# Start-up of a fused attention and MoE kernel: two heads normed first, four weight units loaded first, and an uneven share of W3O

## The chip, the cores and the metric

The kernel runs on one core of a Trainium2 chip. The metric is device time in microseconds (us) of one execution. A core has a matrix engine (TensorE, PE in the profile, with its weight loads as PEld), three elementwise engines (VectorE or DVE, ScalarE or ACT, GpSimd or POOL), and SyncE (SP), whose queue issues nearly all DMA transfers here. Each engine works through its own instructions in a fixed order.

## The reference

```python
q_n, k_n = rmsnorm(q, g_q), rmsnorm(k, g_k)      # q, k, v: (4, 12, 448, 64)
attn = softmax(q_n @ k_n.T / 8)
x = (attn @ v) -> (1792, 768)                    # heads side by side
g = relu(x @ w_in) ** 2                          # w_in 768 x 2048
x = g @ w_out                                    # w_out 2048 x 768
h = ((x @ w1) * (x @ w2)) @ w3                   # w1, w2 768 x 1024, w3 1024 x 1024
out = h @ w_out2                                 # 1024 x 768
```

## The kernel before

The kernel walks over 48 heads (4 batches of 12). `NH`, `H` and `GH` are 48, 12 and 4. For each head it prepares K and Q (`head_prep`, `stage_k`), makes scores in two halves of two 112-row blocks (`stage_qk`), takes the exponential (`stage_exp`), transposes the result (`stage_t`, `stage_lo`) and multiplies by V (`stage_v`). The norms of four heads are made together as a group (`load_group`, `group_prep`); only the first group is cut up. PE would be idle in much of a head, so the loop calls `fill(n)` six times a head, and each call runs matrix products of another job until `n` matmuls are paid for.

During heads 0 to 12 that other job is W3O, the product of w3 and the last weight matrix (`gen_w3o`). It is 8 x 2 x 8 = 128 groups of three matmuls (`mm3`, lines 262 to 264; a high and a low part of each operand make three). From head 13 on it is the MoE chain of the batch whose attention is done, with three such matmuls a group too.

The weights arrive as 64-bit values in units of 128 x 384 or 128 x 512. A unit is loaded by SP (`load_next`, L180) into one of four buffers `raw64`, worked on by ACT (L194) and by POOL or ACT (L200, L198), joined into 32 bits by DVE (L207), which frees the `raw64` buffer, and split into a high part by ACT (L106) and a low part by POOL or, one in five, by DVE (L114). The tiles of a split unit are called `hl`, `x` or `act` in the profile, by the pool that they borrow. The first 16 groups of W3O (`ic` = 0) need 16 units of the last weight matrix (`wo`) and two of w3, a new unit for nearly every group; each 16 groups after them need two units of w3. `advance` keeps loading up to five units ahead of the one in use, as far as the `raw64` buffers allow.

SP's queue is one queue in a fixed order: a load that waits for its buffer holds up all behind it. `qt`, the transposed Q of a head, has two buffers, and a buffer comes free when DVE has made `ql` (L497) of the head that used it.

The scheduler of the framework puts the instructions of each engine into their order when the kernel is built, by the order in the program and by what it expects to be ready, so an instruction can stand earlier or later than its place in the program.

Of the kernel before, what the change touches and what calls it, by code (L numbers as in the profile page):

```python
# [29 lines left out]
def attention_moe_kernel(  # L30
# [15 lines left out]
    nc = tc.nc  # L46
    B, P, H, C, D = q_nat.shape
    S = P * C
    NH = B * H
    GH = 4  # L50
# [5 lines left out]
    NIC = w3t.shape[0] // 2  # L56
# [114 lines left out]
    def is64(i):  # L171
        return units[i][0].dtype != F32
# [14 lines left out]
    def load_to(i):  # L187
        while pos["load"] <= min(i, NU - 1) and is64(pos["load"]):
            load_next()
# [200 lines left out]
    def load_group(g):  # L390
        if not (0 <= g < NH // GH):
            return
        b, h0 = divmod(g * GH, H)
        qn = t1.tile([P, GH, C, D], F32, name="qn", tag="qn")
        kn = t2.tile([P, GH, C, D], F32, name="kn", tag="kn")
        if g == 0:
            nc.sync.dma_start(out=kn[:, 0:1], in_=k_nat[0, :, 0:1])
            load_head(0)
            nc.sync.dma_start(out=qn[:, 0:1], in_=q_nat[0, :, 0:1])
            load_to(0)  # L400
            nc.sync.dma_start(out=kn[:, 1:], in_=k_nat[0, :, 1:GH])
            nc.sync.dma_start(out=qn[:, 1:], in_=q_nat[0, :, 1:GH])
            load_to(1)
        else:
            nc.sync.dma_start(out=kn, in_=k_nat[b, :, h0:h0 + GH])
            nc.sync.dma_start(out=qn, in_=q_nat[b, :, h0:h0 + GH])
        grp[g] = [qn, kn, None, None]

    def load_head(h):
        if not (0 <= h < NH):  # L410
            return
        b, hh = divmod(h, H)
        t = t2.tile([128, S], F32, name="qt", tag="qt")
        nc.sync.dma_start(out=t, in_=q_t[b, hh])
        qts[h] = t
# [22 lines left out]
    def group_prep(g):  # L438
        if not (0 <= g < NH // GH):
            return  # L440
        qn, kn = grp[g][:2]
        n = GH * C
        if g == 0:
            sq = hlp.tile([128, 1024], F32, name="sq", tag="hl")[:P].rearrange("p (h c d) -> p h c d", h=GH, c=C)
        else:
            sq = qn
        ss = small.tile([P, 2, n], F32, name="ss", tag="ss")
        rr = grp[g][2] = t2.tile([P, 2, n], F32, name="rr", tag="rr")

        def sums(i, x, sq, a, b):  # L450
            nc.scalar.activation(out=sq[:, a:b], in_=x[:, a:b], func=AF.Square)
            t = sq[:, a:b].rearrange("p h c d -> p (h c) d")
            nc.vector.tensor_reduce(out=ss[:, i, a * C:b * C], in_=t, axis=AX.X, op=ALU.add)

        def norm(i, j, a, b):
            s = ss[:, i:j, a * C:b * C]
            nc.vector.tensor_scalar(out=s, in0=s, scalar1=1.0 / D, scalar2=1e-6, op0=ALU.mult, op1=ALU.add)
            return rsqrt(rr[:, i:j, a * C:b * C], s)

        if g == 0:  # L460
            sums(1, kn, sq, 0, 1)
            first.enter_context(tc.issue_after(norm(1, 2, 0, 1)))
            head_prep(0)
            stage_k(0)
            sums(0, qn, qn, 0, 1)
            norm(0, 1, 0, 1)
            sums(1, kn, sq, 1, GH)
            sums(0, qn, qn, 1, GH)
            norm(0, 2, 1, GH)
        else:  # L470
            sums(0, qn, qn, 0, GH)
            sums(1, kn, sq, 0, GH)
            norm(0, 2, 0, GH)

    def head_prep(h):
        if not (0 <= h < NH):
            return
        g, i = divmod(h, GH)
        _, kn, rr, _ = grp[g]
        kx = t1.tile([P, C, D], F32, name="kx", tag="kx")  # L480
        nc.gpsimd.tensor_tensor(
            out=kx, in0=kn[:, i], in1=rr[:, 1, i * C:(i + 1) * C].unsqueeze(2).to_broadcast([P, C, D]), op=ALU.mult
        )
        khl = t2.tile([P, C, 2 * D], F32R, name="khl", tag="khl")
        copy_on(KHI_ENG[h // H], khl[:, :, :D], kx)
        sub_on(KLO_ENG[h // H], khl[:, :, D:], kx, khl[:, :, :D].bitcast(F32))
        qt = qts.pop(h)
        qh = t2.tile([128, S], F32R, name="qh", tag="qh")
        ql = t2.tile([128, S], F32R, name="ql", tag="ql")
        qe = QHI_ENG[h // H]  # L490
        if qe == "a":
            nc.scalar.activation(out=qh, in_=qt, func=AF.Copy, scale=gg[:, 0:1])
        else:
            ENGS[qe].tensor_scalar(
                out=qh, in0=qt, scalar1=gg[:, 0:1], scalar2=1.0, op0=ALU.mult, op1=ALU.mult
            )
        nc.vector.scalar_tensor_tensor(  # L497
            out=ql, in0=qt, scalar=gg[:, 0:1], in1=qh.bitcast(F32), op0=ALU.mult, op1=ALU.subtract
        )
        heads[h] = dict(khl=khl, qh=qh, ql=ql, rq=rr[:, 0, i * C:(i + 1) * C], p=[None] * C, pt={}, lo=[])  # L500
# [145 lines left out]
    def start_fill(gen, total):  # L646
        state.update(gen=gen, credit=0.0, left=total)

    def fill(n):
        state["credit"] += n  # L650
        while state["gen"] is not None and state["credit"] > 0:
            try:
                k = next(state["gen"])
                state["credit"] -= k
                state["left"] -= k
            except StopIteration:
                state["gen"] = None

    MOE = 3 * (NFC * KX + 2 * NE * KF + 2 * NJ * KX + NE * NIC)
    W3O = 3 * 2 * NIC * NIC  # L660

    nc.scalar.preload_act_table_set("natural_log_exp_and_others")
    nc.sync.dma_start(out=g_sb, in_=g_in)
    load_group(0)
    load_head(1)
    make_identity(nc, ident)
    nc.vector.tensor_copy(out=ident_r, in_=ident)
    nc.vector.scalar_tensor_tensor(
        out=gg, in0=g_sb[:, 0:1], scalar=float(D) ** -0.5, in1=g_sb[:, 1:2], op0=ALU.mult, op1=ALU.mult
    )  # L670
    first = ExitStack()
    group_prep(0)
    load_head(2)
    head_prep(1)
    load_v(0)
    start_fill(gen_w3o(), W3O)
    first.close()
    for h in range(NH + 1):
        n = W3O / ((H + 1) * 6) if h <= H else MOE / (H * 6)
        load_head(h + 3)  # L680
        load_v(h + 1)
        if h % GH == 0:
            load_group(h // GH + 1)
        stage_qk(h, 0)
        fill(n)
        stage_exp(h, 0)
        if h % H != 1:
            stage_x(h - 2)
        stage_t(h - 1, 0)
        stage_t(h - 1, 1)  # L690
        fill(n)
        stage_lo(h - 1)
        if h < NH:
            v_prep(h)
        fill(n)
        stage_k(h + 1)
        stage_t(h - 1, 2)
        stage_t(h - 1, 3)
        fill(n)
        stage_lo(h - 1)  # L700
        stage_qk(h, 1)
        fill(n)
        stage_exp(h, 1)
        fill(n)
        stage_v(h - 1)
        if h % GH == 1:
            group_prep(h // GH + 1)
        head_prep(h + 2)
        if h and h % H == 0:
            fill(1e9)  # L710
            stage_x(h - 1)
            start_fill(gen_moe(h // H - 1), MOE)
    fill(1e9)
# [56 lines left out]
```

## Time and profile before

| | us |
|---|---|
| median of 3 runs (1233.05 to 1234.97) | 1234.19 |
| the profiled execution | 1230.67 |
| its span (first to last instruction) | 1228.6 |
| PE busy | 1162.9 (95%) |
| POOL busy | 781.5 (64%) |
| ACT busy | 732.0 (60%) |
| DVE busy | 689.0 (56%) |

The profiled execution is one run of its own; 2.07 us of its time lie outside the span. A busy share is an average over stages, and the stages differ: in the first 58.91 us PE is busy for 33.39 us.

### The profile page before, as it was taken

Reading aid. Unit: us, or ns where it says so; the run is one execution under the profiler, and the core shown is the slowest. Engines: PE = TensorE matmul, PEld = TensorE weight load, DVE = VectorE, ACT = ScalarE, POOL = GpSimd, SP = SyncE. Lnnn points to the kernel's source line nnn. Section 1 sums busy time; section 2 is a strip of 40 time slices with the busy share of each in tenths; the row PEclk is TensorE's granted clock in tenths of the full one; section 3 lists DMA queues with packets and bytes.
Section 4 is the critical chain, followed back from the end, with each engine's and each line's share of the span. In section 5 each row is a group of like instructions: output and inputs, shape, how many; then the busy total and the mean of one; then the engine's idle time right before and its main releaser. Section 6 shows DMA issues by size and latency. Waiting matters only on the chain.

```text
span 1228.6 us, 18882 instructions
## 1 busy us (share of the span) xinstructions
PE 1162.9 (95%) x6192; PEld 1050.8 (86%) x6192; DVE 689.0 (56%) x1230; ACT 732.0 (60%) x1581; POOL 781.5 (64%) x772
## 2 busy tenths in 40 slices
PE   4798999997988899999999999999999999999998
PEld 3587888886877799998998999999999999999998
DVE  5798888759978773556566554645655421012100
ACT  6898877767657565656646556656555544443442
POOL 5884425665676664756776664846766556678673
PEclk9799999999999999999999999999999999999999
DMA  7785457888788865545545455444543443333342
GB/s 224 246 256 158 146 148 237 271 290 251 256 254 261 245 192 172 146 131 150 159 114 167 134 168 164 140 133 136 153 123 114 138 138 114 110 113 103 104 125 75
DMA packets 111346, 207.63 MB, mean 169 GB/s; under 512 B 12208, under 2 KB 66704, under 8 KB 111248
## 3 DMA queue, kind: packets, MB, share of 16 engines
q1 hardware_dynamic: 107792, 200.92, 54.2%
q10 hardware_dynamic: 3456, 5.51, 1.2%
q8 instruction: 49, 0.80, 0.3%
q14 instruction: 49, 0.40, 0.1%
HBM read 149.95 MB, written 27.53 MB: 144 GB/s over the span
## 4 chain that ended last, share of the span: by engine, by line
PE 69%; DMA 10%; DVE 8%; ACT 5%; POOL 4%; issue 3%; SPq 1%; DVEq 0%; POOLq 0%; ACTq 0%
PE mm L262 19%; PE mm L263 19%; PE mm L264 19%; PE pt L571 4%; PE kv L623 3%; DMA raw<-w_out 2%; PE sc L525 2%; DMA raw<-w 2%; DMA pw<-p 2%; PE sc L526 2%; ACT p L544 2%; DMA raw<-w_in 2%; DVE nb L527 1%; POOL hl L114 1%; DVE raw L207 1%
## 5 line engine op out<-in xcount | busy, mean ns | idle before, releaser
L114 POOL TENSOR_TENSOR hl<-raw,hl 128x384 fp32r<-128x384 f32 (+1 forms) x383 | 446.3, 1169 | 261.3 <-ACT hl L106 250.8
L106 ACT ACTIVATE hl<-raw 128x384 fp32r<-128x384 f32 (+1 forms) x416 | 233.6, 564 | 148.8 <-PE mm L264 86.4
L262 PE MATMUL mm<-x,hl 128*128 128x448 f32 (+1 forms) x832 | 309.6, 372 | 1.4 <-DVE gf L334 1.4
L263 PE MATMUL mm<-x,hl 128*128 128x448 f32 (+1 forms) x832 | 305.9, 368 | 4.5 <-POOL x L114 4.4
L264 PE MATMUL mm<-x,hl 128*128 128x448 f32 (+1 forms) x832 | 304.9, 366 | 3.4 <-DVE hl L114 1.9
L263 PE MATMUL mm<-act,hl 128*128 128x448 f32 (+1 forms) x640 | 235.8, 368 | 3.2 <-POOL act L114 2.3
L262 PE MATMUL mm<-act,hl 128*128 128x448 f32 (+1 forms) x640 | 238.1, 372 | 0.0
L264 PE MATMUL mm<-act,hl 128*128 128x448 f32 (+1 forms) x640 | 234.5, 367 | 0.7 <-DVE hl L114 0.7
L544 ACT ACTIVATE p<-sc,nb,rr 112x448 f32<-112x448 f32 x192 | 137.5, 720 | 76.6 <-DVE nb L528 74.4
L263 PEld LDWEIGHTS mm<-x,hl 128*128 128x128 f32 x832 | 157.6, 189 | 19.2 <-POOL x L114 7.1
L264 PEld LDWEIGHTS mm<-x,hl 128*128 128x128 f32 x832 | 157.7, 189 | 17.2 <-DVE hl L114 2.3
L262 PEld LDWEIGHTS mm<-x,hl 128*128 128x128 f32 x832 | 157.8, 190 | 15.1 <-DVE gf L334 1.8
L527 DVE TENSOR_REDUCE nb<-sc 112x1 f32<-112x448 f32 x192 | 113.4, 615 | 40.3 <-PE sc L526 38.6
L263 PEld LDWEIGHTS mm<-act,hl 128*128 128x128 f32 x640 | 121.7, 190 | 14.6 <-POOL act L114 4.0
L264 PEld LDWEIGHTS mm<-act,hl 128*128 128x128 f32 x640 | 121.7, 190 | 10.7 <-DVE hl L114 1.1
L262 PEld LDWEIGHTS mm<-act,hl 128*128 128x128 f32 x640 | 121.7, 190 | 9.7
L114 DVE TENSOR_TENSOR ptr<-pt,ptr 128x448 fp32r<-128x448 f32 x144 | 86.8, 619 | 72.8 <-ACT ptr L106 72.0
L200 POOL TENSOR_SCALAR raw<-raw 128x384 uint32<-128x384 uint16 (+1 forms) x110 | 81.2, 739 | 64.5 <-DMA raw<-w_in 23.8
L207 DVE SCALAR_TENSOR_TENSOR raw<-raw 128x384 uint32<-128x384 uint32 (+1 forms) x120 | 82.7, 694 | 42.8 <-POOL hl L114 28.5
L114 POOL TENSOR_TENSOR act<-gf,act 128x448 fp32r<-128x448 f32 x80 | 97.1, 1214 | 7.6 <-ACT act L106 3.4
L194 ACT ACTIVATE raw<-raw 128x384 f32<-128x384 f32 (+1 forms) x120 | 70.6, 599 | 50.8 <-DMA raw<-w 17.6
L334 DVE TENSOR_TENSOR gf<-mm,r 128x448 f32<-128x448 f32 x64 | 39.8, 621 | 96.0 <-ACT r L330 95.4
(84 smaller groups left out, 1578.6 us busy)
## 6 DMA issues: line engine op xcount, KB each, us to landing
pw<-p SPq DMA_DIRECT2D x72, 392.0 KB, 4.3
raw<-f_in SPq DMA_DIRECT2D x96, 192.0 KB, 2.4
raw<-f_out SPq DMA_DIRECT2D x72, 256.0 KB, 2.7
raw<-f SPq DMA_DIRECT2D x96, 192.0 KB, 2.4
raw<-w_in SPq DMA_DIRECT2D x32, 384.0 KB, 4.5
raw<-w_out SPq DMA_DIRECT2D x24, 512.0 KB, 5.9
raw<-w SPq DMA_DIRECT2D x32, 384.0 KB, 5.0
raw<-w3o SPq DMA_DIRECT2D x48, 256.0 KB, 2.8
```

The costliest lines, as they stand in the source:

```text
L106: nc.scalar.activation(out=out, in_=in_, func=AF.Copy)
L114: e.tensor_tensor(out=out, in0=in0, in1=in1, op=ALU.subtract)
L194: nc.scalar.activation(out=hi, in_=hi, func=AF.Prelu, scale=2.0**-112, alpha=-(2.0**32))
L200: nc.gpsimd.tensor_scalar(out=t[:, :n, 0], in0=low, scalar1=2.0**-13, scalar2=2.0**-14 - 0.5, op0=ALU.mult, op1=ALU.add)
L207: nc.vector.scalar_tensor_tensor(out=f[:, :n].bitcast(U32), in0=t[:, :n, 1], scalar=3, in1=t[:, :n, 0], op0=ALU.logical_shift_left, op1=AL ...
L262: nc.tensor.matmul(ps, w[:, 0, wk, :], x[0], start=(i == 0), stop=False)
L263: nc.tensor.matmul(ps, w[:, 0, wk, :], x[1], start=False, stop=False)
L264: nc.tensor.matmul(ps, w[:, 1, wk, :], x[0], start=False, stop=(i == last))
L334: nc.vector.tensor_tensor(out=gf, in0=ps, in1=r, op=ALU.mult)
L527: nc.vector.tensor_reduce(out=nb[:, j:j + 1], in_=o[j], axis=AX.X, op=ALU.max, negate=True)
L544: nc.scalar.activation(out=p, in_=o[j], func=AF.Exp, scale=d["rq"][:, c:c + 1], bias=nb[:, j:j + 1], accum_out=sm[:, i, c:c + 1],)
L571: nc.tensor.transpose(to[:kn, c * P:(c + 1) * P], d["p"][c][:, k0:k0 + kn], one)
```

## The change

In the first group, K and Q of heads 0 and 1 are loaded as one piece and normed together (before: head 0 alone, then heads 1 to 3). The `qt` load of head 1 and the first `wo` unit go ahead of K and Q of heads 2 and 3, and two more `wo` units are loaded right behind those. `head_prep(1)` moves ahead of the norm of the later heads. Head 0 gets no W3O in its first four `fill` calls and four groups in its last two; head 1 gets 8 groups, head 2 gets 9, and heads 3 to 12 get 10.7 each. Before, each of the 13 heads got 9.85.

```diff
         if g == 0:
-            nc.sync.dma_start(out=kn[:, 0:1], in_=k_nat[0, :, 0:1])
+            nc.sync.dma_start(out=kn[:, 0:2], in_=k_nat[0, :, 0:2])
             load_head(0)
-            nc.sync.dma_start(out=qn[:, 0:1], in_=q_nat[0, :, 0:1])
+            nc.sync.dma_start(out=qn[:, 0:2], in_=q_nat[0, :, 0:2])
             load_to(0)
-            nc.sync.dma_start(out=kn[:, 1:], in_=k_nat[0, :, 1:GH])
-            nc.sync.dma_start(out=qn[:, 1:], in_=q_nat[0, :, 1:GH])
+            load_head(1)
             load_to(1)
+            nc.sync.dma_start(out=kn[:, 2:], in_=k_nat[0, :, 2:GH])
+            nc.sync.dma_start(out=qn[:, 2:], in_=q_nat[0, :, 2:GH])
+            load_to(3)
...
         if g == 0:
-            sums(1, kn, sq, 0, 1)
-            first.enter_context(tc.issue_after(norm(1, 2, 0, 1)))
+            sums(1, kn, sq, 0, 2)
+            first.enter_context(tc.issue_after(norm(1, 2, 0, 2)))
             head_prep(0)
             stage_k(0)
-            sums(0, qn, qn, 0, 1)
-            norm(0, 1, 0, 1)
-            sums(1, kn, sq, 1, GH)
-            sums(0, qn, qn, 1, GH)
-            norm(0, 2, 1, GH)
+            sums(0, qn, qn, 0, 2)
+            norm(0, 1, 0, 2)
+            head_prep(1)
+            sums(1, kn, sq, 2, GH)
+            sums(0, qn, qn, 2, GH)
+            norm(0, 2, 2, GH)
...
+    GROUPS = [4, 8, 9] + [(2 * NIC * NIC - 21) / (H - 2)] * (H - 2)
...
     load_group(0)
-    load_head(1)
...
     load_head(2)
-    head_prep(1)
     load_v(0)
...
-        n = W3O / ((H + 1) * 6) if h <= H else MOE / (H * 6)
+        n = 3 * GROUPS[h] / (6 if h else 2) if h <= H else MOE / (H * 6)
...
         stage_qk(h, 0)
-        fill(n)
+        if h:
+            fill(n)
         stage_exp(h, 0)
...
         stage_t(h - 1, 1)
-        fill(n)
+        if h:
+            fill(n)
...
             v_prep(h)
-        fill(n)
+        if h:
+            fill(n)
...
         stage_t(h - 1, 3)
-        fill(n)
+        if h:
+            fill(n)
         stage_lo(h - 1)
         stage_qk(h, 1)
         fill(n)
```

## Rows read from the trace of the kernel before

**Rows 1.** Page, part 2: PE busy tenths in 40 slices of 30.7 us

```profile
PE   4798999997988899999999999999999999999998
```

**Rows 2.** Windows by stage: length, then busy us per engine, clock, DMA share, GB/s

```profile
0.00:12.00 12.00, 0.71 (x4) 0.56 (x4) 6.41 (x18) 6.66 (x14) 3.95 (x11) 1.00 0.80 227
12.00:31.00 19.00, 12.56 (x38) 8.67 (x38) 11.12 (x24) 12.70 (x30) 14.09 (x19) 1.00 0.68 223
31.00:58.91 27.91, 20.12 (x73) 15.62 (x73) 21.40 (x34) 22.79 (x48) 24.01 (x22) 0.76 0.80 256
58.91:72.85 13.94, 13.94 (x85) 12.71 (x85) 13.06 (x23) 12.85 (x30) 12.03 (x14) 1.00 0.84 236
72.85:176.00 103.15, 95.31 (x586) 84.98 (x585) 86.64 (x170) 84.47 (x190) 51.77 (x67) 1.00 0.55 167
```

**Rows 3.** Waits of POOL from 7 to 59 us: total, times, longest

```profile
POOL raw L200 <- DMA raw<-wo: 4.1, 3, 1.7
POOL hl L114 <- ACT hl L106: 3.0, 2, 1.5
```

**Rows 4.** Timeline of SP's queue from 4 to 32 us: start, duration, what

```profile
4.00 0.43 SPq L180 DMA_DIRECT2D raw<-wo  x1
...
8.26 0.43 SPq L405 DMA_DIRECT2D kn<-k_nat  x1
13.48 0.34 SPq L414 DMA_DIRECT2D qt<-q_t  x1
...
14.34 1.38 SPq L180 DMA_DIRECT2D raw<-wo  x3
15.81 0.38 SPq L180 DMA_DIRECT2D raw<-w3t  x1
25.19 2.70 SPq L180 DMA_DIRECT2D raw<-wo  x3
```

**Rows 5.** Timeline of DVE from 4 to 17 us

```profile
4.20 0.42 DVE L453 TENSOR_REDUCE ss<-sq 112x4 f32<-112x256 f32 x1 [1.53 <-ACT sq L451]
...
9.68 0.95 DVE L453 TENSOR_REDUCE ss<-sq 112x12 f32<-112x768 f32 x1
...
12.78 0.68 DVE L497 SCALAR_TENSOR_TENSOR ql<-qt,gg,qh 128x448 fp32r<-128x448 f32 x1
13.37 1.25 DVE L431 TENSOR_TENSOR nt<-rr 112x24 f32<-112x24 f32 x1
...
16.12 0.18 DVE L435 TENSOR_TENSOR rr<-nt,rr 112x24 f32<-112x24 f32 x1
```

**Rows 6.** Timeline of POOL from 13 to 31 us

```profile
13.20 1.38 POOL L114 TENSOR_TENSOR hl<-raw,hl 128x512 fp32r<-128x512 f32 x1 [1.55 <-ACT hl L106]
...
19.07 0.72 POOL L114 TENSOR_TENSOR khl<-kx,khl 112x256 fp32r<-112x256 f32 x1
...
30.24 0.53 POOL L200 TENSOR_SCALAR raw<-raw 128x384 uint32<-128x384 uint16 x1 [1.21 <-DMA raw<-wo]
```

**Rows 7.** Timeline of PE from 9 to 73 us

```profile
9.70 0.71 PE L509 MATMUL kv<-ident_r,khl 112*128 112x112 f32 x4 [9.70 <-DVE ident_r L667]
...
19.84 0.74 PE L509 MATMUL kv<-ident_r,khl 112*128 112x112 f32 x4 [1.65 <-POOL khl L114]
20.38 0.69 PE L526 MATMUL sc<-kt,ql 128*112 128x448 f32 x1
...
36.54 0.52 PE L262 MATMUL mm<-act,hl 128*128 128x384 f32 x1
36.86 0.52 PE L263 MATMUL mm<-act,hl 128*128 128x384 f32 x1
...
58.22 0.33 PE L264 MATMUL mm<-act,hl 128*128 128x384 f32 x1
58.39 0.33 PE L262 MATMUL mm<-act,hl 128*128 128x384 f32 x1
...
72.85 0.36 PE L525 MATMUL sc<-kt,qh 128*112 128x448 f32 x1
```

**Rows 8.** Timeline of ACT from 3 to 17 us

```profile
3.75 0.42 ACT L451 ACTIVATE sq<-kn 112x256 f32<-112x256 f32 x1 [1.74 <-DMA kn<-k_nat]
...
8.81 0.84 ACT L451 ACTIVATE sq<-kn 112x768 f32<-112x768 f32 x1
...
16.61 0.72 ACT L544 ACTIVATE p<-sc,nb,rr 112x448 f32<-112x448 f32 x1 [0.53 <-DVE nb L528]
```

**Rows 9.** Waits of PE from 0 to 100 us, the longest but one

```profile
PE sc L525 <- ACT p L544: 3.8, 3, 2.2
```

## The prediction

> **What bounds the kernel now.** I began with the page's row of PE by slices [rows 1]. PE is at nine tenths or more almost everywhere; the first two slices stand out with four and seven. So the kernel is bound by PE except at its start, and a change at the start can win only what PE loses there.
>
> Then I cut the start into stages by windows [rows 2]. Up to 12 us PE has nothing to do, from 12 to 31 us it is busy 12.56 of 19.00 us, and from 31 to 58.91 us 20.12 of 27.91. From 58.91 us on, where the scores of head 2 begin, it is full (13.94 of 13.94), and from 72.85 us (scores of head 3, the last row of [rows 7]) to 176.00 us (scores of head 12) it has 95.31 of 103.15. So 58.91 − 33.39 = 25.5 us of PE are idle before head 2. The busy part is slow as well: in heads 0 and 1 a matmul of 384 columns follows the one before after 0.32 us (36.54 to 36.86), at 58 us after 0.17 (58.22 to 58.39) [rows 7], and the granted clock was 0.76 over 31 to 58.91 us [rows 2], a mixture of the two levels 1.2 and 2.4 GHz.
>
> Which engine is late there? POOL is the busiest from 31 to 58.91 us, 24.01 us or 86% [rows 2], and it is on the conversion of weight units: of what it waited for from 7 to 59 us, 4.1 us were loads of `wo` units and 3.0 us high parts from ACT [rows 3]. The queue that issues these loads says why they are late [rows 4]. After the unit at 4.00 us none goes out until 14.34. From 8.69 us the queue stands at the `qt` load of head 3, which needs the buffer that head 1's `ql` frees at 13.46 [rows 5]; the next three units follow it, one w3 unit at 15.81, and then again none until 25.19. Head 1 is late for a related reason: its norm is the tail of the long norm over heads 1 to 3, done at 16.30 us [rows 5], its K is split by 19.79 [rows 6], and PE waits for it at 19.84 while head 0's second half of scores stands behind it at 20.38 [rows 7].
>
> **The change, part by part.** I make the sum against the profiled execution (1230.67 us, that is 1228.6 of span and 2.07 around it) and carry the difference to the median of the runs, 1234.19, which is 3.52 above it.
>
> *Loads two units ahead.* The second and third `wo` units leave at about 4.9 and 5.4 us in place of 14.34 and later. Eleven loads precede the `qt` load of head 2 instead of nine, and cost no path that I see: heads 2 and 3, V and the second group wait 768 KB longer, 2.8 us at 284 GB/s (an estimate: 227 GB/s at a DMA share of 0.80 in the first window [rows 2]), and none of them is needed before 16 us. With head 1 normed first, its `ql` no longer has to wait, and the queue passes the `qt` load of head 3 several us earlier; every later unit load stands behind that one. What goes is POOL's waiting for `wo` loads: 4.1 us. Below: nothing, if the same waits come back one unit later. Above: 4.1 + 3.0 = 7.1 us, with the waits for the high parts. I take **4.1 us**, since only the loads are touched.
>
> *Fewer groups in heads 0 to 2.* The first 16 groups are those that need a unit each. Before they end 16 − 9.85 = 6.15 groups into head 1, that is after 1.62 heads; now after 4 + 8 = 12 groups two heads are through and 4 of 9 groups of head 2, after 2.44. So 0.82 heads of attention more fit under the time in which POOL converts those units. A head costs PE 95.31 / 9 = 10.59 us [rows 2], less 9.85 groups x 3 x 0.174 = 5.14 us (spacing at the full level), so 5.45 of attention, and 0.82 of it is 4.5 us. Below: nothing, if the other engines leave no room. For 0.82 heads DVE needs at most 0.82 x 86.64 / 9 = 7.9 us and has 46.91 − 32.52 = 14.4 free from 12 to 58.91 us, ACT 7.7 of 11.4 [rows 2]; 4.1 us fewer if the first term is won. That just fits, but in a fixed order of instructions seldom without gaps. I take half, **2.2 us**. The waits that come next are those of scores for their PSUM buffers behind the exponential [rows 9].
>
> *The groups that moved.* 9.85 x 3 − 21 = 8.54 groups, 8.54 x 3 x 0.174 = 4.46 us of PE, move to heads 3 to 12, 0.45 us each. They are not a loss of their own: after the first 16 groups 112 are left before and after. If the earlier heads don't get shorter, they become one (the first rival). No engine's other work changes in amount.
>
> *Two heads normed at once.* On the path to head 0 K's piece is 224 KB in place of 112 (0.4 us at the rate above). The square is 0.42 us for 256 columns and 0.84 for 768, so 0.63 for 512; the sum is 0.42 and 0.95, so 0.68 [rows 5, 8]. That is 0.4 + 0.21 + 0.26 = 0.9 us on the path to PE's first work at 9.70 us. Below: nothing, because head 0's first exponential at 16.61 us [rows 8] waited for the norms of the later heads, which move behind it. I take **0.9 us** against.
>
> *The later norm.* Its small DVE steps now run among POOL's splits. At 13.37 us such a step took 1.25 us while a split of 1.38 us ran on POOL from 13.20 [rows 5, 6]. Heads 2 and 3 are not needed before head 0 is done, so I count nothing; uncovered, four such steps would cost at most 5 us for head 2. The Trainium skill ("GPSIMD Engine Reference", section 1, Specifications) says that GpSimd shares its SBUF interfaces with VectorE and that VectorE instructions with two SBUF inputs contend for them. The row agrees, with 1.25 us. By that rule the later norm alone would add an estimated 1.1 us or so per step and the sum would lose at most a part of it; I leave it out of the sum.
>
> Sum: 4.1 + 2.2 − 0.9 = 5.4 us faster. The profiled execution would be 1225.3 us, the median **1228.8 us**.
>
> **The rivals.**
>
> *The heads set the pace, not the units (slower).* If heads 0 to 2 are held by their own chain (scores, maximum, exponential, transposes), then head 3 starts its scores at 72.85 us as now, and 4.46 us of groups that PE did on the side have to be done among heads 3 to 12, where 7.84 us of 103.15 are idle [rows 2]. Nothing absorbed gives 1234.19 + 4.46 = 1238.7 us. It decides itself at 72.85 − 4.46 = 68.4 us: only when head 3 starts before that, the shift pays. For it speaks that PE waited 3.8 us for the exponential to free score buffers [rows 9]; against it POOL's 86% and its waits for loads. Chance 0.12.
>
> *POOL's own work is the limit (no change).* From 31 to 58.91 us only 3.9 us of POOL are free [rows 2]. If its order of work only moves the waits, the first two terms shrink to about 1 us and pay for the norm's 0.9: 1234.2 us. Against it: 4.9 us idle from 12 to 31 us. Chance 0.18.
>
> *Everything fits (much faster).* 7.1 + 4.5 and nothing for the norm: 11.6 us, 1222.6. It takes DVE and ACT without gaps from 12 us on, which their rows only just allow. Chance 0.15.
>
> *The clock stays down.* With fewer groups in the first two heads PE does less there. At the low level a matmul is spaced by 0.32 in place of 0.174 us [rows 7]; over 12 groups that is 12 x 3 x 0.146 = 5.3 us. PE is mostly waited for by no one in that stage, so half of it on the path, 2.6 us, gives 1231.4. The Trainium skill ("TensorE: Matmul & The Clock Gate", Part 1: The HAM clock gate) says that the throttled clock is the default and that activity releases it. By that rule removing PE work from the first heads speaks against the change. The trace agrees in that the clock fell to 0.76 in the stage with 28% idle. Chance 0.08.
>
> **How the numbers follow.** The forecast of 1228.8 us has the remaining 0.47; its own range, with 0 to 7.1, 0 to 4.5 and 0.9 to 0, the ends not all together, is 1224 to 1232. The range of 8 in 10 takes in most of "everything fits" and the middle of the slower case, in which part is absorbed: 1222.5 to 1236.5. A measurement of this kernel tells 0.2%, 2.5 us, from no change, so faster is below 1231.7. From the forecast 0.45, all of "everything fits" 0.15, 0.05 of the clock's case and 0.05 of POOL's, together 0.70; the slower rival gives 0.11; the rest, 0.19, is the same.
>
> **What would show it.** Right: the second and third `wo` loads out before 7 us; head 1's K transposes at 14 to 16 us in place of 19.84; no pause in unit loads like those from 4.00 to 14.34 and 15.81 to 25.19; POOL's waits for `wo` loads below 2 us; head 3's scores at 72.85 − 4.46 − 5.4 = 63.0 us; PE still busy at least 92% from there to head 12. Wrong: head 3 after 68.4 us; a new long wait on ACT or DVE before 20 us for K or Q of heads 2 and 3, which land later; or a start as forecast with the time given back from head 3 to head 12.

## The result and the profile after

The changed kernel took 1238.56 us (median of 11 runs, 1235.71 to 1241.82). The kernel before took 1233.05 us beside it (11 runs, 1228.37 to 1235.41). The ratio is 1.0052 with a 95% interval of 1.0037 to 1.0067: slower by half a per cent, where 0.4% faster was forecast. The slower rival had put the time at 1238.7, from a baseline that was 1.1 us higher. The profiled execution took 1239.43 us, its span is 1237.7. The two profiled executions lie 8.8 us apart and the medians 5.5, so the rows below overstate the loss.

The page of the kernel after, busy time of PE, and its row by slices with the granted clock:

```profile
PE 1167.5 (94%) x6192; PEld 1056.1 (85%) x6192; DVE 688.3 (56%) x1230; ACT 731.4 (59%) x1581; POOL 778.4 (63%) x772
...
PE   3798999898898899999999999999999999999998
...
PEclk9699999999999999999999999999999999999999
```

Against [rows 1] the first slices are no fuller, and there are eights where there were nines. Windows of the kernel after, first by the stages of [rows 2], then split where head 12 begins its scores:

```profile
0.00:12.00 12.00, 0.00 (x0) 0.00 (x0) 5.47 (x17) 5.82 (x11) 3.31 (x10) 1.00 0.79 227
12.00:31.00 19.00, 11.87 (x42) 8.37 (x42) 11.58 (x24) 13.06 (x29) 15.95 (x21) 0.93 0.67 206
31.00:58.91 27.91, 20.90 (x67) 15.27 (x68) 17.86 (x34) 23.51 (x52) 18.54 (x20) 0.68 0.75 237
58.91:72.85 13.94, 12.26 (x57) 10.47 (x55) 10.84 (x17) 7.65 (x19) 12.87 (x15) 0.76 0.73 221
...
0.00:185.15 185.15, 146.69 (x778) 126.44 (x778) 134.55 (x266) 139.15 (x307) 104.08 (x131) 0.91 0.62 185
185.15:1300.00 1114.85, 1020.85 (x5415) 929.67 (x5415) 553.73 (x965) 592.27 (x1275) 674.27 (x641) 0.99 0.52 156
```

The last two rows say where to look. Head 12 starts at 185.15 us in place of 176.0, which is 9.15 later, and the profiled execution as a whole is 8.8 longer: the loss of these two executions is complete by head 12. After it PE is busy for 1020.85 us, before the change 1162.9 − 142.64 = 1020.3 (142.64 being the sum of the five stages of [rows 2]). Up to head 12 PE is busy 146.69 us in place of 142.64 and idle 185.15 − 146.69 = 38.46 us in place of 33.36, with about the same matmuls. In the stage from 31 to 58.91 us POOL has 18.54 us of work where it had 24.01: it has less done by 58.91 us and more gaps.

Some of what was foreseen did come. The queue of SP in the kernel after, as [rows 4]:

```profile
5.34 1.31 SPq L180 DMA_DIRECT2D raw<-wo  x2
...
12.32 0.33 SPq L407 DMA_DIRECT2D kn<-k_nat  x1
16.07 0.33 SPq L408 DMA_DIRECT2D qn<-q_nat  x1
16.50 0.38 SPq L180 DMA_DIRECT2D raw<-wo  x1
16.96 0.38 SPq L180 DMA_DIRECT2D raw<-w3t  x1
17.92 11.44 SPq L180 DMA_DIRECT2D raw<-wo  x3
```

The second and third `wo` units go out by 6.65 us. Then nothing of weights goes out until 16.50: the queue no longer stands at a `qt` load but at the Q of the second group (heads 4 to 7, L408), whose one buffer comes free only with DVE's last sum over the Q of the first group, that of heads 2 and 3. DVE in the kernel after, as [rows 5]:

```profile
15.36 0.69 DVE L455 TENSOR_REDUCE ss<-qn 112x8 f32<-112x512 f32 x1 [1.68 <-ACT qn L453]
```

The buffer is free at 16.05 us, and the load leaves at 16.07. It is a stop of the old kind in a new place.

Waits of POOL from 7 to 59 us in the kernel after, as [rows 3]:

```profile
POOL hl L114 <- ACT hl L106: 3.7, 1, 3.7
...
POOL raw L200 <- DMA raw<-wo: 1.2, 1, 1.2
```

The waits for `wo` loads fell from 4.1 to 1.2 us, as forecast, while those for high parts rose from 3.0 to 3.7, and head 3 is late all the same. Timeline of PE in the kernel after, as [rows 7]:

```profile
13.49 0.73 PE L512 MATMUL kv<-ident_r,khl 112*128 112x112 f32 x4 [13.49 <-POOL khl L114]
14.86 0.71 PE L528 MATMUL sc<-kt,qh 128*112 128x448 f32 x1 [0.63 <-ACT kt L106]
...
16.49 0.65 PE L512 MATMUL kv<-ident_r,khl 112*128 112x112 f32 x4
...
75.08 0.44 PE L528 MATMUL sc<-kt,qh 128*112 128x448 f32 x1
```

PE's first work is at 13.49 us in place of 9.70, head 1's K at 16.49 in place of 19.84 (14 to 16 forecast), and head 3 begins at 75.08 in place of 72.85, where 63.0 was forecast and 68.4 was named as the point from which the change loses.

### The profile page after: what moved, and what is told of

It is laid out like the page before. It is cut to its first block, busy times and chain, and to the rows that moved or that the text cites. A ratio compares the mean times of both kernels' runs of the same rounds, so it can differ in the third digit from the quotient of the medians.

```text
span 1237.7 us, 18888 instructions
## 1 busy us (share of the span) xinstructions
PE 1167.5 (94%) x6192; PEld 1056.1 (85%) x6192; DVE 688.3 (56%) x1230; ACT 731.4 (59%) x1581; POOL 778.4 (63%) x772
## 4 chain that ended last, share of the span: by engine, by line
PE 62%; DMA 8%; DVE 4%; ACT 3%; issue 2%; POOL 2%; SPq 0%; DVEq 0%; ACTq 0%; POOLq 0%
PE mm L262 18%; PE mm L263 18%; PE mm L264 17%; PE kv L626 3%; DMA raw<-w 3%; PE pt L574 3%; DMA pw<-p 3%; PE sc L529 1%; PE sc L528 1%; DVE raw L207 1%; POOL hl L114 1%; DMA raw<-w_in 1%; ACT p L547 1%; DMA raw<-w_out 1%; DVE nb L530 1%
## 5 line engine op out<-in xcount | busy, mean ns | idle before, releaser
L207 DVE SCALAR_TENSOR_TENSOR raw<-raw 128x384 uint32<-128x384 uint32 (+1 forms) x120 | 89.6, 750 | 44.4 <-POOL hl L114 30.2
```

The lines of the kernel that those rows point to most:

```text
L207: nc.vector.scalar_tensor_tensor(out=f[:, :n].bitcast(U32), in0=t[:, :n, 1], scalar=3, in1=t[:, :n, 0], op0=ALU.logical_shift_left, op1=AL ...
```

## The experiments

The theories to be told apart were these. Theory A: the new order of loads and norms, with its late first work of PE, carries the loss. Theory B: the uneven shares alone carry it, because the moved groups have to be done among the later heads. Theory D, from E5 on, is B in a wider form: the first heads take as long as they take, groups in them are done beside what they wait for, and groups moved out of them are simply owed. Further ones came up on the way: theory C, that a group not done in the first heads also delays the conversion of the unit it would have used; theory E, that a stop in head 6 is the loss; theory F, that the new stop of SP is; theory G, that the late first work of PE is. Each ratio is to the kernel before on the same chip. E1 to E4 shared one chip, and so did E5 to E8, E9 to E12, E13 to E16, and E17 with E18. In none is any of the computation left out.

### E1: the uneven shares alone

```diff
  (kernel before)
+    GROUPS = [4, 8, 9] + [(2 * NIC * NIC - 21) / (H - 2)] * (H - 2)
-        n = W3O / ((H + 1) * 6) if h <= H else MOE / (H * 6)
+        n = 3 * GROUPS[h] / (6 if h else 2) if h <= H else MOE / (H * 6)
-        fill(n)            # the first four of the six
+        if h:
+            fill(n)
```

> The kernel before with the uneven shares of W3O alone (4, 8, 9, then 10.7 groups); loads and norms as before. Theory A (the loss is the late first work of PE: the norm of two heads and the new load order): PE starts at 9.7 us as before, no loss, 1231 to 1236 us. Theory B (the moved groups are the loss, 4.46 us among heads 3 to 12 and a longer stall of VectorE in head 6): slower by 4 to 7 us, ratio 1.003 to 1.006, and VectorE's longest wait for a join in head 6 grows from 2.9 to about 5 us.

Measured: 1237.62 us, 1.0050 [1.0038, 1.0062]. The shares alone lose as much as the whole change, as theory B expected. The profiled execution is the slowest of the six (1241.70 of 1236.12 to 1241.70), so its rows overstate the loss. Windows of E1 up to head 12, then from head 3 to head 12:

```profile
0.00:183.50 183.50, 145.05 (x778) 124.55 (x778) 139.27 (x266) 139.43 (x307) 105.15 (x131) 0.95 0.62 187
...
74.00:183.50 109.50, 100.78 (x613) 91.36 (x611) 88.02 (x175) 88.30 (x197) 51.29 (x66) 0.97 0.55 158
```

Head 3 begins at 74.0 us: with 8.54 groups fewer before it, it is no earlier than at 72.85 [rows 7]. PE is idle 74.0 − (145.05 − 100.78) = 29.7 us before it, against 25.5 [rows 2]. The groups had stood in holes of the first heads; the holes stayed.

### E2: two heads normed at once, alone

```diff
  (kernel after, shares as before)
-            load_to(3)
```

> The loads and norms of two heads first, without the two extra units and with even shares of W3O. Theory A: PE's first work moves from 9.7 to 12 to 13.5 us and the kernel loses 3 to 5 us, ratio 1.002 to 1.004. Theory B: head 1 is ready earlier and the kernel is level or up to 3 us faster, ratio 0.997 to 1.000.

Measured: 1234.58 us, 1.0030 [1.0018, 1.0042]. PE's first work is at 14.23 us, 4.5 later than in [rows 7]. The second w3 unit, which the next groups need, leaves SP at 18.66 us and is joined only at 36.18, where the kernel before has it at 30.8. Theory A had expected a loss of this kind.

### E3: two units loaded sooner, alone

```diff
  (kernel before)
-            load_to(1)
+            load_to(3)
```

> The kernel before with only the two more units of the last weight matrix loaded in the first group. Theory A: as POOL's order at the start stays, PE still starts near 9.7 us; level, ratio 0.998 to 1.002. The forecast's first term (POOL's 4.1 us of waiting for such loads goes away) would give 0.997. Theory B says nothing of this part and expects it level.

Measured: 1237.92 us, 1.0058 [1.0045, 1.0071]. The term forecast at 4.1 us of gain is a loss of its own on the old start. Waits of POOL from 7 to 59 us in E3:

```profile
POOL hl L114 <- ACT hl L106: 6.5, 2, 5.8
...
POOL raw L200 <- DMA raw<-wo: 2.8, 2, 1.5
```

The waits for `wo` loads fell by 1.3 us against [rows 3], the waits for high parts rose by 3.5. The `qt` load of head 3 leaves at 18.87 us where it left at 13.48 [rows 4], and the next unit behind it at 19.32. Head 1 begins its scores at 29.84 us in place of 25.23 and head 3 at 82.11 in place of 72.85, so the loss is made in the first heads. Why that costs 0.58% was not settled.

### E4: the change without the shares

```diff
  (kernel after)
-        n = 3 * GROUPS[h] / (6 if h else 2) if h <= H else MOE / (H * 6)
+        n = W3O / ((H + 1) * 6) if h <= H else MOE / (H * 6)
         # and all six calls of fill(n) in head 0 as before
```

> The changed kernel with even shares of W3O (9.85 groups for each head). Theory A: the late start stays, 1.003 to 1.006 as for the whole change. Theory B: the loss goes away, ratio 0.996 to 1.001, and VectorE's wait in head 6 is back at 2 to 3 us.

Measured: 1231.24 us, 1.0003 [0.9991, 1.0016]. The other parts together are neutral: on the new start the two units gain 0.27% (E2 to E4) and pay for the norm. With E1 this puts the loss on the shares, on either start. E4's profiled execution is its slowest, 1237.94 of 1229.52 to 1237.94, so its rows overstate its time.

### E5: the conversions at an even pace

Theory C: units are converted when the groups that need them come up, so taking groups out of head 0 delays its units too. In the kernel after the last of the first 18 units is joined at 54.51 us, before the change at 50.69. The edit calls for the units of heads 0 and 1 at six even steps a head, whatever the groups.

```diff
  (kernel after)
+    def convert(h):
+        if h < 2:
+            even["k"] += 1
+            g = min(int(128 / 78 * even["k"]) + 1, 16)
+            advance(min(g + (g > 4), 15))
...
+        convert(h)         # ahead of each of the six fill calls
```

> The changed kernel, with its uneven shares of W3O, but the conversion of the first units stands in the program where the even shares had put it (a call that only advances the units, at each of the six places of heads 0 and 1). Theory C (a unit's conversion stands in the program just ahead of the group that uses it, so fewer groups in heads 0 to 2 put the conversions of the first 18 units behind more attention work on ACT, DVE and POOL, and the last of them, which everything waits for, come later): head 3 starts before 70 us in place of 75.1, ratio 0.998 to 1.001. Theory D (the heads' own chain sets the start, and the moved groups are simply owed): head 3 stays at 73 to 76 us, ratio 1.004 to 1.006.

Measured: 1232.06 us, 0.9982 [0.9968, 0.9996]. The loss is gone; that unit is joined at 50.75, and head 3 begins at 70.8 us, where theory C had expected it before 70 and theory D from 73 on. Waits of PE from 14 to 76 us, in the kernel after and then in E5:

```profile
PE mm L263 <- POOL x L114: 8.6, 5, 2.7
```

```profile
PE mm L263 <- POOL x L114: 3.9, 5, 1.2
```

Without the even pace PE stands 8.6 us at groups whose low parts POOL has not made; with it 3.9. Taken alone this would make theory C the whole cause. E10 and E13 were made to test that.

### E6 and E7: the joins of later weights held back

In head 6 the kernel after has a stop of DVE and PE. Timeline of DVE, then of PE, in the kernel after:

```profile
118.67 1.60 DVE L207 SCALAR_TENSOR_TENSOR raw<-raw 128x384 uint32<-128x384 uint32 x1 [5.44 <-POOL hl L114]
```

```profile
115.46 0.35 PE L262 MATMUL mm<-x,hl 128*128 128x384 f32 x1
115.65 0.34 PE L263 MATMUL mm<-x,hl 128*128 128x384 f32 x1
...
116.00 1.19 PE L626 MATMUL kv<-ptr,vhl 128*128 128x448 f32 x5
121.48 0.74 PE L626 MATMUL kv<-ptr,vhl 128*128 128x448 f32 x1 [4.29 <-DVE ptr L114]
...
122.67 0.52 PE L262 MATMUL mm<-x,hl 128*128 128x384 f32 x1
122.99 0.52 PE L263 MATMUL mm<-x,hl 128*128 128x384 f32 x1
```

The scheduler put the join of a `w_in` unit, which is not needed before head 13, ahead of attention work on DVE. It waits 5.44 us for a 32-bit buffer that POOL's split of a w3 unit frees, and the attention behind it waits too, PE among it for 4.29 us. The kernel before has the same stop, shorter (2.0 us of PE), and E1 has it with the same 5.44 us on DVE. Theory E: this is the loss. The edit holds such joins until the last split of attention on DVE has been issued, in the kernel after (E6) and in the kernel before (E7).

```diff
+        with tc.issue_after(held["ins"]) if i >= U0 and held else ExitStack():
             nc.vector.scalar_tensor_tensor(...)      # the join, L207
...
-            sub_on("v", lo, p, hi)                   # in stage_lo
+            held["ins"] = nc.vector.tensor_tensor(out=lo, in0=p, in1=hi, op=ALU.subtract).ins
```

> The changed kernel, with the joins of the MoE units on VectorE held behind the attention work that stands ahead of them in the program. Theory E (a large part of the loss is one stop in head 6, where a join that overtook attention work waits 5.4 us for its buffer with all of VectorE behind it, and PE loses 4.3 us and then its clock): the stop goes away, 4 to 6 us come back, ratio 1.000 to 1.002. Theory D: the groups are owed whatever stops there, ratio 1.004 to 1.006.

> The same hold of the joins in the kernel before, as the control of e6. Its stop there is 2.9 us on VectorE and 2.0 us on PE. Theory E: 1 to 2 us faster, ratio 0.998 to 1.000. If holding the joins helps by itself as much as it helps the changed kernel, e6 says nothing of the change.

Measured: E6 1236.81 us, 1.0029 [1.0010, 1.0048]; E7 1226.93 us, 0.9945 [0.9921, 0.9968]. The stop is gone in both. The hold gains more in the kernel before, where the stop is the shorter one, than in the kernel after, so the stop is not what the change lost. The edit holds every such join of the whole kernel, so its gain is not the price of this one stop. E7 beats both kernels by a change that has nothing to do with the start.

### E8: more groups early instead of fewer

```diff
  (kernel after, all six fill calls in head 0)
+    GROUPS = [12, 12, 12] + [(2 * NIC * NIC - 36) / (H - 2)] * (H - 2)
```

> The changed kernel's loads and norms with the shares the other way round: 12 groups for each of heads 0 to 2, in all six places, and 9.2 for each later head. Theory D (groups in the first heads are done beside what those heads wait for anyway): 1 to 4 us faster than the kernel before, ratio 0.997 to 0.999. Theory C: the first units are converted earlier, the same sign. If instead the first heads are paced by the units and nothing else, more groups there cost as much as they save, ratio 1.000 to 1.003.

Measured: 1233.1 us, 0.9984 [0.9972, 0.9996]. If each group moved cost its PE time, the 36 − 29.5 = 6.5 groups would gain 6.5 x 3 x 0.174 = 3.4 us, 0.27%; against E4 it is 0.19%, from another chip, and the intervals overlap.

### E9: without the new stop of SP

The second group's K and Q are loaded at head 1, behind the next units (theory F).

```diff
  (kernel after)
-        if h % GH == 0:
+        if h == 1 or h and h % GH == 0:
             load_group(h // GH + 1)
```

> The changed kernel with the loads of the second group's K and Q one head later in the program, so that SP's queue does not stand before its Q (whose one buffer VectorE frees only with the sum over the first group's Q, at 16 us) with the next weight units behind it. Theory F (this new stop took the place of the one removed, and cancels the gain of the earlier units): the fifth unit leaves near 11.5 us in place of 16.5, its join comes at 22 to 25 us in place of 28.5, head 3 starts 2 to 4 us earlier, ratio 1.001 to 1.003. Rival (POOL's order, which has K of heads 2 and 3 ahead of those units, holds them anyway): the unit leaves earlier, but the joins of units 4 to 6 stay at 28 to 31 us and the ratio at 1.004 to 1.006.

Measured: 1237.53 us, 1.0044 [1.0021, 1.0067]. The next unit leaves at 12.39 us in place of 16.50 and is joined at 24.84 in place of 28.46, and head 3 begins at 71.98, 3.1 us earlier, as theory F expected; but the ratio is that of the whole change within its interval, where 1.001 to 1.003 was expected. The stop is real, and removing it gains nothing that can be told from no change (the interval leaves room for 0.3%): theory F falls as the cause of the loss.

### E10 and E11: the even pace on the old start

E10 is E1 with the calls of E5, E11 the kernel before with them, as the control.

```diff
  (kernel before; E10 also the shares of E1)
+        convert(h)         # ahead of each of the six fill calls
```

> The uneven shares alone on the loads and norms of before (as e1), with the units converted at the even pace (as e5). Theory C: the loss of e1 (1.005) goes away whatever the start is, ratio 0.997 to 1.001, and the last unit of the first eighteen is joined within 1 us of 50.7. Theory D: ratio stays at 1.004 to 1.006.

> Control: the same calls that only convert units, in the kernel before with its even shares, where they ask for what the group behind them asks for anyway. Theory C: no change, ratio 0.998 to 1.002. If the calls help by themselves by 0.5% or more, e5 and e10 show nothing of the shares.

Measured: E10 1237.06 us, 1.0031 [1.0017, 1.0044]; E11 1230.6 us, 0.9984 [0.9964, 1.0004]. On the old start the shares lose 0.47% although the conversions run at the same even pace. Theory C is not the whole cause, and theory D's 1.004 to 1.006 was not met either. In E1 the last of the 18 units is not late (its join begins at 49.42 us, 50.69 before); the one behind it, of w3, is (54.49 in place of 51.79), and in E10 it is joined at 52.12. Head 3 begins at 69.1 us in E10 and at 74.0 in E1: the pace does shorten the first heads here too, and half of that is given back by head 12 (180.8 and 183.5 us).

### E12: even pace and held joins together

```diff
  (kernel after)
+        convert(h)                                   # as in E5
+        with tc.issue_after(held["ins"]) if i >= U0 and held else ExitStack():   # as in E6
```

> The whole change with both mends: units at the even pace (e5, 0.998) and the joins of the MoE units held behind attention work (e7, 0.9945). If the two add up, ratio 0.991 to 0.994 and the fastest of all; if the hold only helps where the start is late, about 0.997.

Measured: 1228.44 us, 0.9963 [0.9949, 0.9978]. The gains that the two edits had on the changed kernel (0.70% in E5, 0.23% in E6) add up; the 0.991 to 0.994 expected from E7's larger gain was not reached, and E7, with none of the change in it, is not beaten.

### E13: even shares with the even pace on the new start

```diff
  (E5)
-        n = 3 * GROUPS[h] / (6 if h else 2) if h <= H else MOE / (H * 6)
+        n = W3O / ((H + 1) * 6) if h <= H else MOE / (H * 6)
```

> The changed kernel's loads and norms with even shares of W3O (as e4) and the calls that convert the first units at the even pace (as e5). Theory C (the uneven shares lose because they pull the units late; with the units at the even pace they cost nothing): no faster than e5, ratio 0.997 to 1.000. Theory D (the moved groups are owed among the later heads, 0.36%, whatever the units do, and the calls help by themselves): faster than e5 by 0.3 to 0.5%, ratio 0.993 to 0.996.

Measured: 1229.99 us, 0.9980 [0.9966, 0.9993], against 0.9982 for E5. With the even pace on the new start the shares cost nothing. Windows from head 3 to head 12, of E13 and then of E5:

```profile
75.60:176.90 101.30, 94.31 (x582) 84.94 (x582) 86.50 (x170) 84.97 (x190) 52.30 (x66) 1.00 0.56 166
```

```profile
70.80:178.70 107.90, 98.06 (x603) 87.68 (x601) 91.40 (x174) 87.67 (x197) 59.77 (x73) 1.00 0.56 166
```

The first heads did get shorter, by 4.8 us to head 3, and the next nine longer by 6.6: the shift paid at the front and was given back.

### E14 and E16: more groups early on the old start

E14 is the kernel before with the shares of E8, E16 that with the held joins of E7.

```diff
  (kernel before)
+    GROUPS = [12, 12, 12] + [(2 * NIC * NIC - 36) / (H - 2)] * (H - 2)
-        n = W3O / ((H + 1) * 6) if h <= H else MOE / (H * 6)
+        n = 3 * GROUPS[h] / 6 if h <= H else MOE / (H * 6)
```

> The kernel before with 12 groups in each of heads 0 to 2 and 9.2 in each later head, nothing else. Theory D: 6.45 groups of 0.52 us, 3.4 us, are done beside the first heads' waiting: ratio 0.996 to 0.999. If the even shares of before are where both stages balance, 1.000 to 1.003.

> Shares of 12, 12, 12 and 9.2 (as e14) with the joins held (as e7). If both gains add up, the fastest: ratio 0.990 to 0.993. If the first heads have no more room for groups, as e7: 0.994 to 0.997.

Measured: E14 1231.15 us, 0.9990 [0.9976, 1.0004]; E16 1225.69 us, 0.9956 [0.9938, 0.9975]. Neither is told apart from its partner with even shares (1, and E7's 0.9945). Fewer early loses, more early gains some 0.2% at most: that fits first heads which hold about as many groups as they can at the even share.

### E15: the shares where the stop is held back

```diff
  (E1)
+        with tc.issue_after(held["ins"]) if i >= U0 and held else ExitStack():   # as in E7
```

> The uneven shares alone (as e1) on the kernel with the joins held (e7, 0.9945). It has no stop of VectorE in head 6, so what the shares cost here is the owed groups alone. Theory D: 0.3 to 0.45% above e7, ratio 0.997 to 0.999. Theory E (most of e1's loss is the stop in head 6): within 0.15% of e7, ratio 0.993 to 0.996.

Measured: 1237.09 us, 1.0034 [1.0018, 1.0050], against 0.9945 for E7: the shares cost 0.9% with no stop in head 6 left, so theory E falls. That is twice the 0.3 to 0.45% that theory D expected. Scores of head 3 and head 12 and the windows, first of E7, then of E15:

```profile
72.59 0.36 PE L527 MATMUL sc<-kt,qh 128*112 128x448 f32 x1
...
173.75 0.46 PE L527 MATMUL sc<-kt,qh 128*112 128x448 f32 x1 [0.27 <-ACT p L546]
```

```profile
0.00:173.75 173.75, 141.71 (x779) 121.49 (x779) 136.63 (x261) 137.12 (x302) 103.27 (x127) 0.96 0.60 183
...
72.60:173.80 101.20, 95.32 (x583) 84.71 (x582) 85.85 (x165) 82.28 (x185) 50.09 (x63) 1.00 0.47 142
```

```profile
72.70 0.44 PE L527 MATMUL sc<-kt,qh 128*112 128x448 f32 x1
...
178.99 0.46 PE L527 MATMUL sc<-kt,qh 128*112 128x448 f32 x1 [0.78 <-ACT p L546]
```

```profile
0.00:178.99 178.99, 142.89 (x777) 123.01 (x777) 138.18 (x262) 137.50 (x302) 102.91 (x126) 0.97 0.60 177
...
72.70:179.00 106.30, 98.90 (x613) 89.63 (x611) 90.08 (x171) 86.69 (x192) 48.71 (x61) 1.00 0.50 139
```

Head 3 starts at the same time, 72.59 and 72.70 us. From there E15 has 30 matmuls more (613 and 583), which at 0.174 us are 5.2, and takes 5.1 us longer. These nine heads had 5.9 us of idle PE in E7 and have 7.4 now: the idle time did not take the added work. That is the first half of the loss. The spans differ by 9.8 us (1235.6 and 1225.8), so 4.6 us are lost after head 12, and the rows here do not show why.

### E17 and E18: PE's first work

In the kernel after POOL converts the low words of a `wo` unit (0.86 us from 11.40) just ahead of head 0's K split, which PE waits for. Theory G: this delays everything. E17 holds that conversion behind the split. E18 puts all that helped together: even shares, even pace, held joins and this.

```diff
+            with tc.issue_after(prep["ins"]) if i == 1 else ExitStack():
                 nc.gpsimd.tensor_scalar(...)         # low words, L200
...
+        if h == 0:
+            prep["ins"] = split                      # head 0's K split on GpSimd
```

> The changed kernel with one instruction held: POOL converts the low words of the first unit of the last weight matrix only behind its split of head 0's K. In the changed kernel that conversion stands ahead of the split and waits 1.16 us for its load, and PE's first work is at 13.49 us. Theory G (this order makes the larger part of the late start): PE starts at 11 to 11.6 us and the kernel is 1 to 3 us faster than the whole change, ratio 1.002 to 1.004. Rival (the start is hidden behind the units, which come at the same time): PE starts as early, the ratio stays at 1.004 to 1.006.

> The changed kernel's loads and norms without its shares, and with the three holds that helped or may help: units at the even pace (e13, 0.998), late joins (e7, 0.9945) and head 0's K split first. If they add up, 0.990 to 0.993 and the fastest; if the new start has nothing to give, as e7 and e16, 0.994 to 0.997.

Measured: E17 1237.84 us, 1.0051 [1.0032, 1.0069]; E18 1228.29 us, 0.9965 [0.9947, 0.9982]. Timeline of PE in E17:

```profile
11.20 0.74 PE L517 MATMUL kv<-ident_r,khl 112*128 112x112 f32 x4 [11.20 <-POOL khl L492]
14.43 0.72 PE L533 MATMUL sc<-kt,qh 128*112 128x448 f32 x1 [2.50 <-ACT kt L106]
```

The transposes come 2.3 us earlier, the scores 0.4 (14.86 before): ACT, in its fixed order, squares the late K of heads 2 and 3 and makes a high part ahead of `kt`. Theory G falls. E18 agrees with E12, which has the uneven shares and not the last hold (0.9965 and 0.9963): a second case in which the shares cost nothing with the even pace on the new start. It does not beat E7: no run shows a gain from the new start itself.

## Why the prediction was wrong

**The step that failed** is "Fewer groups in heads 0 to 2" (2.2 us of gain), together with the sentence on "The groups that moved" that they "are not a loss of their own". The first three heads were taken to be as long as POOL needs for the first 16 units, so that fewer groups in them would let 0.82 heads more through. In place of that gain the shares lose 0.50% alone (E1), 0.9% against E7 (E15) and 0.49% against E4 (the whole change); only with the even pace on the new start do they lose nothing. PE had 25.5 us idle before head 3 with the groups in; with 8.54 groups taken out it has about as much (1.2 us less to 4.2 more), and they come back in heads whose idle time doesn't take them. Five pairs of profiles, with and without the shares, the rest alike; PE's idle time is the length of a stretch less PE's busy time in it, in us:

| pair (even, uneven shares) | head 3 starts | head 12 starts | PE idle up to head 3 | PE idle from 3 to 12 | ratios to before |
|---|---|---|---|---|---|
| before, E1 | 72.8, 74.0 | 176.0, 183.5 | 25.5, 29.7 | 7.8, 8.7 | 1, 1.0050 |
| E7, E15 (held joins) | 72.6, 72.7 | 173.8, 179.0 | 26.2, 28.7 | 5.9, 7.4 | 0.9945, 1.0034 |
| E4, after | 79.0, 75.1 | 180.3, 185.2 | 28.8, 29.5 | 6.4, 9.0 | 1.0003, 1.0052 |
| E11, E10 (even pace) | 76.8, 69.1 | 177.5, 180.8 | 27.5, 27.0 | 6.2, 11.0 | 0.9984, 1.0031 |
| E13, E5 (even pace) | 75.6, 70.8 | 176.9, 178.7 | 25.7, 24.5 | 7.0, 9.8 | 0.9980, 0.9982 |

In the first two pairs, on the old start without the even pace, head 3 is no earlier, as in the rival "The heads set the pace, not the units", and at head 12 the loss is 7.5 and 5.2 us where it had 4.46. But it is not for the rival's reason, since heads 0 and 1 do get shorter: head 2 begins at 51.87 us in E1 in place of 58.91, and at 52.16 in E15 in place of 58.67. Head 2 then takes all of it back. PE was full there before (13.94 of 13.94 us); the windows of head 2 in E1 and then in E15, and the longest waits of PE in that window of E1:

```profile
51.87:73.96 22.09, 16.53 (x71) 13.38 (x70) 18.00 (x27) 15.05 (x32) 18.79 (x19) 0.77 0.65 210
```

```profile
52.16:72.70 20.54, 15.33 (x71) 12.94 (x70) 16.01 (x27) 13.81 (x30) 17.61 (x18) 0.82 0.69 226
```

```profile
PE mm L263 <- POOL x L114: 1.8, 2, 1.1
PE mm L264 <- POOL hl L114: 1.5, 1, 1.5
```

With DVE's low parts (0.8 us) and ACT's high parts (0.6) 4.7 of PE's 5.6 idle us in E1 are at W3O groups whose operands are not split yet, not at the head's own chain. The busy part is slower too: 71 matmuls take 16.53 us, at a granted clock of 0.77, where 85 took 13.94 at 1.00. So the first heads wait for the units also with fewer groups in them; 21 groups up to head 3 still need all of the first 18 units. With the even pace (E10) PE is idle for 1.3 us in head 2, and head 3 does come earlier.

In the last three pairs head 3 is 3.9 to 7.7 us earlier (the 3.9 us from E4's slowest execution), so fewer groups can shorten the first heads; but the later heads, whose 7.84 us of idle PE I took for room, grow by 6.6 to 11.0 us, and their idle time rises in every pair. In the kernel after PE is busy 101.13 of 110.10 us there, 91.9%, just under the 92% forecast, but of a longer stage: the time given back from head 3 to head 12 that the prediction named as a way to be wrong. Up to head 12 the uneven shares lose in all five, by 1.8 to 7.5 us. The rival's bound, "head 3 before 68.4 us", was the right kind of test: none of the five reached it (E10 came nearest, with 69.1).

**Loads two units ahead**, forecast at 4.1 us of gain: the loads went out before 7 us and POOL's waits for `wo` loads fell below 2 us, both as foreseen. On the new start the step is worth 0.27%, 3.3 us (E2 to E4), near the forecast; on the old start it loses 0.58% (E3). The forecast that no pause in the unit loads would be left was wrong; a new one stands at the Q of heads 4 to 7, and by E9 removing it gains nothing measurable.

**Two heads normed at once**, forecast at 0.9 us against: PE's first work moved by 3.8 us, from 9.70 to 13.49, and the step alone loses 0.30%, 3.7 us (E2). The size was off by a factor of four. Of the 3.8 us 2.3 are POOL's order, with a low-word conversion ahead of head 0's K split, and E17 takes them away without a gain. That E2 joins its second w3 unit only at 36.18 us was seen, not tested, as a reason. "The later norm", costed at nothing, cannot be told apart from it; one of its small steps was slow (0.97 us, last section).

**The rivals.** The slower one came about in its time, and that its 1238.7 us meets the 1238.56 so closely is luck: the measured difference is 5.5 us, from a lower baseline, and the units do set the pace of head 2. On the new start the loss comes and goes with the pace of the conversions (E5 against the kernel after). "POOL's own work is the limit" does not hold, since POOL is busy for 18.54 of 27.91 us in that stage and the time is longer. "The clock stays down" is seen in part: the granted clock from 31 to 58.91 us is 0.68 in place of 0.76, and PE's busy time up to head 12 rose by 4.05 us of the 9.15. But in E15 PE's busy time up to head 12 is only 1.2 us above that of E7, of 5.2 us lost there, and in E10 it is 1.1 us below that of E11 (142.75 and 143.81) with 3.3 lost, so the clock is no condition of the loss.

**What stays open.** Why head 3 comes earlier on the new start also without the even pace, and on the old start only with it; why the heads from 3 on take longer than the added work; why the two units alone lose on the old start; and why E1 and E15 lose 3.8 and 4.6 us more after head 12. So that the shares carry the loss is shown by the runs, and how they do is shown in part. Each edit makes the scheduler order the whole kernel anew, and a single comparison below some 0.3% carries that; the table rests on the sign of five pairs, each profile being one run, of which those of E1 and E4 are the slowest of their kernels. E7, which only holds the later joins back, and E16 are the fastest kernels here (0.9945 and 0.9956).

## What to carry to other kernels

Filler work in a stage where the bounding engine has holes can be close to free there; before moving it out, ask what else will fill the holes, and take the idle time of the stage that receives it for room only if a row shows that its holes can be filled. Where filler drags other work with it (here the conversion of its operands), moving the one moves the other, so pace them apart before judging either. And a fixed order of instructions can put work that is due much later ahead of work that is due now: look for a long wait of an engine at an instruction that nobody needs yet.

## What the runs showed of the hardware

After 4.29 us without work (E6 and E7 above) the spacing of 384-column matmuls on PE went from 0.19 us (115.46 to 115.65) to 0.32 (122.67 to 122.99), that is to the low level of the clock in the middle of the kernel: such a stop costs again in the matmuls behind it. The granted clock of the windows before and behind the stop, in the kernel after, went from full to half:

```profile
110.00:117.20 7.20, 7.14 (x44) 6.18 (x42) 3.23 (x6) 7.08 (x17) 6.14 (x11) 1.00 0.61 185
...
121.48:124.00 2.52, 2.52 (x7) 2.11 (x8) 2.49 (x6) 0.57 (x1) 0.32 (x1) 0.50 0.88 277
```

The Trainium skill ("TensorE: Matmul & The Clock Gate", Part 1: The HAM clock gate) says that the low clock is what an idle engine falls back to, and the rows agree.

The granted clock is no sure guide at the start of the kernel. [rows 2] has 1.00 from 12 to 31 us, while 384-column matmuls follow each other there after 0.32 us, the spacing of the low level. PE in the kernel before:

```profile
27.66 0.52 PE L264 MATMUL mm<-x,hl 128*128 128x384 f32 x1
27.98 0.52 PE L262 MATMUL mm<-act,hl 128*128 128x384 f32 x1
```

In the kernel after, a step of DVE over 112 x 16 numbers took 0.97 us while a split of 1.36 us ran on POOL, and the same kind of step 0.16 us a microsecond later. DVE, then POOL:

```profile
17.34 0.55 DVE L207 SCALAR_TENSOR_TENSOR raw<-raw 128x384 uint32<-128x384 uint32 x1
17.81 0.97 DVE L433 TENSOR_TENSOR nt<-rr 112x16 f32<-112x16 f32 x1
...
18.97 0.16 DVE L434 TENSOR_TENSOR nt<-nt,ss 112x16 f32<-112x16 f32 x1
```

```profile
17.39 1.36 POOL L114 TENSOR_TENSOR x<-raw,x 128x384 fp32r<-128x384 f32 x1
```

The slow step ends 0.03 us after the split, and the slow step of [rows 5] (13.37 us) 0.04 us after the split of [rows 6] (13.20 us). The join that began 0.05 us ahead of the split took 0.55 us, as elsewhere. It looks as if a step that begins during such a split waits for its end; two cases do not prove it.
